# Second feed-forward: seven block products in place of eight in its second product

## The chip, the cores and the metric

One core of one Trainium2 chip runs the whole program in a single launch. The metric is the device time of that launch in microseconds (us): three runs of the kernel before took 784.38, 786.24 and 786.41 us, median 786.24.

## The reference

Three stages run one after the other on 2304 tokens (4 batches of 576) of width 512. The first is windowed and dilated attention, the second a feed-forward with a cosine. The third is the one that matters here:

```python
def _moe2_ref(x, w1, w2, w3, w_out):          # x 2304 x 512, w1..w3 512 x 768, w_out 768 x 512
    h = np.maximum(np.maximum(x @ w1, x @ w2), x @ w3)
    return (h @ w_out).astype(np.float32)
```

Below, "the second feed-forward" is this function, "its first product" is the three products with w1, w2 and w3, and "its second product" is `h @ w_out`.

## The kernel before, in words

Every float32 operand of a matmul is split into two rounded parts, hi and lo, and a product takes three passes: hi x hi, lo x hi, hi x lo (`PASSES`, L445). ScalarE makes hi by a cast (`CAST`), VectorE makes lo by a subtraction; the helper `split` (L636) issues both. Each VectorE, ScalarE and TensorE queue runs its instructions in the order that a scheduler gave them when the program was built, so an instruction that waits holds up all that stand behind it on its engine.

The second feed-forward (`ff2`, L893) works on three blocks `t` of 768 tokens, cut into two halves of 384 (`HALF`). The 768 hidden features are six chunks of 128, taken in pairs: `f` = 0, 1, 2 is a pair, `r` = 0, 1 a chunk of it. Per block there are nine steps `q`, three per pair (one for each of w1, w2, w3).

- First product (`product`, L775). Each step is a 2 x 2 block product (two chunks of features, two halves of tokens) and is already done by seven block products in place of eight: sums A11, S1 ... of weight blocks, sums B11, T1 ... of input blocks, results gathered in the PSUM banks X, V and Y (`SUMS`, L611). Each of the seven is 6 matmuls of 128x384. `post` and `put` take them out of PSUM: ScalarE copies `s` and `v`, VectorE adds and takes the maximum in `mx`. After the third weight of a pair, `put` splits the maximum into a tile `g`, one for each chunk and token half (L818).
- Second product (`acc2`, L840). Output features are four groups `dm` of 128. For each `dm`, each token half `n` and each pair `f`, six matmuls of 128x384 (two chunks, three passes) accumulate in one of the banks 94 to 97 of the built program. That is 24 steps of 6 matmuls per block: 4 x 2 x 3. After the last pair ScalarE copies the bank to `o` and a DMA writes it out (L854). The first three steps fill holes in the block's last step `q`; the other 21 stand alone. While they run, ScalarE and VectorE make the next block's B sums (`b_make`, tiles `bt` and `ring`).
- Weights of the second product. `o_weights` (L743) loads a raw pair of chunks (512 KB, tile `raw`) into free slots of the weight pool and splits each chunk into a tile `w`. The scheduler places these six splits in the last part of the first feed-forward.

The first feed-forward ends with `acc_chunk` (L547, matmuls at L551), which reads the tiles `gt`: ScalarE casts their hi (L214), VectorE subtracts their lo (L542). These tiles come from the pool `gp`, which has two buffers (tag `g`).

Of the kernel before, what the change touches and what calls it, by code (L numbers as in the profile page):

```python
# [8 lines left out]
F32 = mybir.dt.float32  # L9
F32R = mybir.dt.float32r  # L10
# [4 lines left out]
ALU = mybir.AluOpType  # L15
# [3 lines left out]
B, H, S, D = 4, 8, 576, 64  # L19
# [12 lines left out]
NF2 = FF2 // 128  # L32
# [7 lines left out]
HALF = 384  # L40
# [124 lines left out]
def body(  # L165
# [11 lines left out]
    nc = tc.nc  # L177
# [45 lines left out]
    acc = bank[:4]  # L223
# [220 lines left out]
    g = {}  # L444
    PASSES = ((0, 0), (1, 0), (0, 1))  # L445
# [225 lines left out]
    def a_part(q, n):  # L671
        if q >= NB2 * NQUAD:
            return
        cols = 256 * len(PARTS[n])
        made = q < NQUAD and q not in PRE
        dt = F32R if made else F32
        if n < 3:
            w = slot_tile(3 + n + q % 2 * 3, [128, 2, cols], dt, "wa")
        else:
            w = wx.tile([128, 2, cols], dt, tag="x", name="wa")  # L680
        if made:
            if n == 0:
                x = raws[q][:, 0]
            elif n == 3:
                x = raws.pop(q)[:, 1, 256:]
            else:
                x = sums[q].rearrange("p a n -> p (a n)")[:, 512 * n - 512 : 512 * n]
            split(w, x, nc.gpsimd)
            kept[q, n] = w.bitcast(F32)
        else:  # L690

            nc.sync.dma_start(out=w, in_=kept_at(q % NQUAD, n))
            w = w.bitcast(F32R)
        for k, name in enumerate(PARTS[n]):
            ops.setdefault(q, {})[name] = w[:, :, 256 * k : 256 * k + 256]
# [45 lines left out]
    wo = {}  # L741

    def o_weights(f):  # L743

        if f % 2 == 0:
# [43 lines left out]
    taken = {}  # L789
    mx = {}  # L790
    g2 = {}
# [7 lines left out]
    def put(q, r, n, name, to):  # L799

        f, j = QUADS[q % NQUAD]
        x = bank_of(q)[to][:, :HALF]
        if j == 0 and (f, r) not in mx:
            mx[f, r] = slot_tile(10 + f % 2 * 2 + r, [128, 2, HALF], F32, "mx")
        m = mx[f, r][:, n]
        if name is None:
            if j == 0:
                nc.scalar.copy(m, x)
            else:
                nc.vector.tensor_tensor(out=m, in0=x, in1=m, op=ALU.max)  # L810
        else:
            y = taken.pop((q, name))
            o = m if j == 0 else y
            nc.vector.tensor_tensor(out=o, in0=y, in1=x, op=ALU.add)  # L814
            if j:
                nc.vector.tensor_tensor(out=m, in0=m, in1=y, op=ALU.max)  # L816
        if j == 2:
            g = slot_tile(14 + f * 4 + r * 2 + n, [128, 2, HALF], F32R, "g2")  # L818
            split(g, m, nc.vector)
            g2[f, r, n] = g  # L820
            if (r, n) == (1, 0):
                del mx[f, 0], mx[f, 1]

    def post(q, p):
        if p == 1:
# [11 lines left out]
        if p == 4:  # L837
            put(q, 1, 0, None, "X")

    def acc2(t, dm, n, f):  # L840

        a = acc[(2 * dm + n) % 4][:, :HALF]
        for r in range(2):
            for k, (x, y) in enumerate(PASSES):
                nc.tensor.matmul(  # L845
                    a,
                    wo[2 * f + r][:, x, 128 * dm : 128 * dm + 128],
                    g2[f, r, n][:, y],
                    start=f == 0 and r == 0 and k == 0,
                    stop=f == NF2 // 2 - 1 and r == 1 and k == 2,  # L850
                )
        if f == NF2 // 2 - 1:
            o = ptp.tile([128, HALF], F32, tag="pt", name="o")
            nc.scalar.copy(o, a)  # L854
            t0 = (2 * t + n) * HALF
            nc.sync.dma_start(out=outT[dm, :, t0 : t0 + HALF], in_=o)
# [93 lines left out]
    at = [0, 0, 0, 0, 0]  # L950
# [61 lines left out]
    n = len(first)  # L1012
# [347 lines left out]
```

## Time and profile before

| what | value |
|---|---|
| median of three runs | 786.24 us (784.38 to 786.41) |
| the profiled execution, its own time | 783.48 us |
| its span, first to last instruction | 781.7 us |
| TensorE (PE) busy | 757.8 us (97%) |
| VectorE (DVE) busy | 537.7 us (69%) |
| ScalarE (ACT) busy | 429.1 us (55%) |
| mean granted TensorE clock | 0.998 |
| second product, matmuls (L845) | 432, busy 76.3 us |
| first product, matmuls (L780) | 1134, busy 198.7 us |

The profile is of one execution; all durations below come from it. Matmuls are pipelined, so the time of one is read from the step between neighbours and not from its own 334 ns. The second feed-forward runs from about 504 us to the end.

### The profile page before, as it was taken

What the parts mean: (1) busy time and instruction counts of PE and PEld (TensorE: products, weight loads), DVE (VectorE), ACT (ScalarE), POOL (GpSimd) and SP (SyncE); (2) the same over time, 40 slices, a digit from 0 to 9 for tenths busy, and PEclk for the clock granted to TensorE, in tenths of its full rate; (3) what the DMA queues carried; (4) which work ended last, traced back from release to release, by engine and by line L of the source; (5) the groups of instructions that cost most, each with busy time, mean ns of one, the idle gap of its engine ahead of it and who ended that gap; (6) DMA issues with size and microseconds to landing.
All of it is one profiled execution on the core that took longest, in us unless ns stands there. A gap on an engine that the chain in (4) does not pass through costs nothing.

```text
span 781.7 us, 13197 instructions
## 1 busy us (share of the span) xinstructions
PE 757.8 (97%) x4592; PEld 668.4 (86%) x4592; DVE 537.7 (69%) x1416; ACT 429.1 (55%) x1046; POOL 114.4 (15%) x114
## 2 busy tenths in 40 slices
PE   7788999999999999999999999999999999999997
PEld 6566878778878778877788889999999999999997
DVE  6999998876875787677877759955463555625540
ACT  7879999678763767664544535533343332433311
POOL 2334231411121101100112212000200000000000
PEclk9999999999999999999999999999999999999999
DMA  9983111342333543223646562487755878368702
GB/s 347 417 323 123 36 58 51 103 151 97 123 120 133 163 137 118 97 79 115 213 178 209 212 229 112 156 281 243 260 182 165 257 242 257 100 194 254 241 13 81
DMA packets 60402, 134.28 MB, mean 172 GB/s; under 512 B 6704, under 2 KB 21168, under 8 KB 60336
## 3 DMA queue, kind: packets, MB, share of 16 engines
q1 hardware_dynamic: 60336, 133.44, 51.0%
q8 instruction: 36, 0.59, 0.3%
q14 instruction: 30, 0.25, 0.1%
HBM read 101.17 MB, written 32.24 MB: 171 GB/s over the span
## 4 chain that ended last, share of the span: by engine, by line
PE 68%; DVE 14%; DMA 7%; ACT 5%; issue 2%; POOL 2%; SPq 1%; POOLq 0%; DVEq 0%; ACTq 0%
PE bank L780 25%; PE bank L452 15%; PE bank L551 14%; PE bank L845 9%; DMA rawp<-wd 2%; PE bank L341 2%; ACT e L291 2%; PE bank L410 2%; DVE wx L263 2%; DVE e L385 2%; PE bank L393 1%; POOL lo L735 1%; DMA raw<-wd 1%; DMA x1d<-o 1%; DMA opd<-hi 1%
## 5 line engine op out<-in xcount | busy, mean ns | idle before, releaser
L452 PE MATMUL bank<-ring,w 128*128 128x512 f32 (+1 forms) x960 | 218.6, 374 | 2.7 <-ACT ring L214 2.7
L551 PE MATMUL bank<-gt,w 128*128 128x512 f32 (+1 forms) x960 | 216.7, 372 | 3.5 <-DVE o L564 1.8
L780 PE MATMUL bank<-ring,wa 128*128 128x384 f32 x1134 | 198.7, 334 | 0.0
L551 PEld LDWEIGHTS bank<-gt,w 128*128 128x128 f32 x960 | 166.4, 189 | 35.7 <-DVE o L564 2.5
L780 PEld LDWEIGHTS bank<-ring,wa 128*128 128x128 f32 x1134 | 196.6, 188 | 0.4 <-ACT s L796 0.4
L452 PEld LDWEIGHTS bank<-ring,w 128*128 128x128 f32 x960 | 165.5, 189 | 35.6 <-ACT ring L214 3.5
L291 ACT ACTIVATE r<-r,hpi 128x512 f32<-128x512 f32 (+1 forms) x80 | 54.6, 683 | 54.6 <-DVE r L531 25.2
L291 ACT ACTIVATE e<-e,m 96x128 f32<-96x128 f32 x192 | 75.0, 393 | 4.4 <-DVE m L351 4.2
L845 PE MATMUL bank<-g,w 128*128 128x384 f32 x432 | 76.3, 334 | 0.0
L845 PEld LDWEIGHTS bank<-g,w 128*128 128x128 f32 x432 | 75.0, 188 | 0.0
L814 DVE TENSOR_TENSOR s<-s,bank 128x384 f32<-128x384 f32 x36 | 20.0, 554 | 49.0 <-PE bank L780 49.0
L796 ACT COPY s<-bank 128x384 f32<-128x384 f32 x54 | 25.9, 482 | 48.1 <-PE bank L780 47.9
L351 DVE CUSTOM_DVE_ANT_0 e<-bank,cs 96x128 f32<-96x128 f32 x192 | 42.7, 281 | 12.3 <-PE bank L341 12.2
L291 ACT ACT_TABLE_LOAD x38 | 48.8, 1283 | 1.4 <-PEq L1346 0.7
L507 POOL TENSOR_TENSOR gt<-r,gt 128x512 fp32r<-128x512 f32 x25 | 35.6, 1423 | 65.7 <-DVE gt L214 35.8
L210 POOL TENSOR_SCALAR gt<-r 128x512 fp32r<-128x512 f32 x25 | 16.4, 656 | 175.4 <-PE bank L551 117.1
L638 ACT CAST g<-mx 128x384 fp32r<-128x384 f32 x36 | 18.6, 516 | 41.6 <-DVE mx L816 26.8
L282 POOL TENSOR_TENSOR w<-wx,w 128x512 fp32r<-128x512 f32 x23 | 31.5, 1375 | 54.2 <-DVE w L214 45.2
L255 ACT ACTIVATE wh<-wh 128x256 f32<-128x256 f32 x48 | 20.7, 433 | 32.9 <-DMA wh<-in_w 20.5
L385 DVE TENSOR_TENSOR e<-e,z 96x512 f32<-96x512 f32 x48 | 36.8, 796 | 1.0
L291 ACT ACTIVATION_READ_ACCUMULATOR e<-e,m 96x1 f32 x192 | 36.4, 189 | 0.0
L496 DVE TENSOR_TENSOR r<-bank,r 128x512 f32<-128x512 f32 x47 | 32.2, 684 | 5.5 <-ACT r L291 5.3
(83 smaller groups left out, 856.6 us busy)
## 6 DMA issues: line engine op xcount, KB each, us to landing
wa<-opd SPq DMA_DIRECT2D x72, 512.0 KB, 4.5
qkv<-in_qkv SPq DMA_DIRECT2D x48, 336.0 KB, 4.2
wh<-in_w SPq DMA_DIRECT2D x36, 256.0 KB, 2.8
w<-in_w_in SPq DMA_DIRECT2D x16, 512.0 KB, 8.6
w<-in_w_out SPq DMA_DIRECT2D x16, 512.0 KB, 9.2
wa<-opd SPq DMA_DIRECT2D x24, 256.0 KB, 4.3
wd<-wh SPq DMA_DIRECT2D x36, 128.0 KB, 1.8
opd<-hi SPq DMA_DIRECT2D x18, 256.0 KB, 2.1
```

The costliest lines, as they stand in the source:

```text
L255: nc.scalar.activation(high, high, AF.Prelu, scale=2.0**-112, alpha=2.0**32)
L282: eng.tensor_tensor(out=w[:, 1, :], in0=words.pop(key), in1=w[:, 0, :].bitcast(F32), op=ALU.subtract)
L291: last_table.append(nc.scalar.activation(*args, **kw).ins)
L351: nc.vector.tensor_tensor_reduce(out=e[:, 2 * j + h, :], in0=places_of[j, h], in1=mask[:, kind, :], scale=-1.0 / math.sqrt(D), scalar=3e38 ...
L385: eng.tensor_tensor(out=e, in0=e, in1=z[:, n, :].unsqueeze(2).to_broadcast([QB, 4, KB]), op=ALU.mult)
L452: pe(nc.tensor.matmul(hv, w[:, a, 128 * c : 128 * c + 128], ring[c][:, x, c0 : c0 + n_tok], start=n == 0 and j == 0, stop=n == NC - 1 and ...
L496: nc.vector.tensor_tensor(out=r, in0=hv, in1=r, op=ALU.mult)
L507: eng.tensor_tensor(out=gt[:, 1, :], in0=r, in1=gt[:, 0, :].bitcast(F32), op=ALU.subtract)
L551: pe(nc.tensor.matmul(a_dm, w[:, a, 128 * dm : 128 * dm + 128], gt[:, x, :], start=first and n == 0, stop=last and n == 2,))
L780: nc.tensor.matmul(out, ops[q][a][:, x, 128 * c : 128 * c + 128], b_op(b, c)[:, y], start=first and c == 0 and n == 0, stop=c == 1 and n == 2,
L796: nc.scalar.copy(x, bank_of(q)[to][:, :HALF])
L845: nc.tensor.matmul(a, wo[2 * f + r][:, x, 128 * dm : 128 * dm + 128], g2[f, r, n][:, y], start=f == 0 and r == 0 and k == 0, stop=f == NF2 ...
```

## The change

For the pairs `f` = 0 and 1 the second product is also a 2 x 2 block product: two halves of the 512 output features by two token halves, over the two chunks. It now goes by seven block products, each for two groups `m` of 128 output columns. The third pair is done as before and is added in the same banks.

Three things come with it. Sums of the blocks of `w_out` (S1 to S4) are made on chip, once, in `o_weights`, from a raw tile that now sits in the pool `gp`. Sums T1 to T4 of the blocks of `h` are made in every block by `g_sum`, at the places of `G_AT`. And `acc2` now has steps of two kinds: `P1` to `P7` are the seven products, `Lin` is the third pair for output half `i` and token half `n`. After some steps a bank is taken out of PSUM while it is still in use: `P1`, `P5`, `P6` are copied to `taken` by ScalarE, `P7` is added to the copy of `P5` by VectorE, and `L00`, `L01`, `L11` add a `taken` tile to the bank on VectorE. `L10` is a ScalarE copy.

```diff
     def o_weights(f):
+        wo[f] = slot_tile(26 + f, [128, 2, 512], F32R, "w")
+        k, r = divmod(f, 2)
+        raw = raws["o"]
+        if k not in SEVEN:
+            split(wo[f], raw[:, r], nc.vector)
+            return
...
+            split2(of("A11"), a11)
+            s1 = sp.tile([128, 256], F32, tag="e", name="ws")
+            nc.vector.tensor_tensor(out=s1, in0=a21, in1=a22, op=ALU.add)
+            split2(of("S1"), s1)
+            nc.vector.tensor_tensor(out=a21, in0=a11, in1=a21, op=ALU.subtract)
+            split2(of("S3"), a21)
+            nc.vector.tensor_tensor(out=a11, in0=s1, in1=a11, op=ALU.subtract)
+        else:
+            split(wo[f], raw[:, 1], nc.vector)
...
+            split2(of("S2"), a11)
+            nc.vector.tensor_tensor(out=a12, in0=a12, in1=a11, op=ALU.subtract)
+            split2(of("S4"), a12)
+    def o_load(f):
         if f % 2 == 0:
-            raws["o"] = slot_tile(22 + f // 2, [128, 2, 512], F32, "raw")
+            raws["o"] = gp.tile([128, 2, 512], F32, tag="g", name="raw")
             nc.sync.dma_start(out=raws["o"], in_=wod[f // 2])
-        wo[f] = slot_tile(26 + f, [128, 2, 512], F32R, "w")
-        split(wo[f], raws["o"][:, f % 2], nc.vector)
...
+    def split2(hl, x):
+        nc.scalar.copy(hl[0], x)
+        nc.vector.tensor_tensor(out=hl[1], in0=x, in1=hl[0].bitcast(F32), op=ALU.subtract)
+    SEVEN = (0, 1)
...
         if j == 2:
-            g = slot_tile(14 + f * 4 + r * 2 + n, [128, 2, HALF], F32R, "g2")
-            split(g, m, nc.vector)
-            g2[f, r, n] = g
+            if f in SEVEN:
+                name = f"B{r + 1}{n + 1}"
+                g_raw[f, name] = m
+                if name != "B12":
+                    g_op[f, name] = g_tile(f, r * 2 + n)
+                    split2(g_op[f, name], m)
+            else:
+                g2[f, r, n] = g_tile(f, r * 2 + n)
+                split2(g2[f, r, n], m)
...
+    G_AT = ((3, -1), (3, -2), (4, -1), (4, -2), (6, -2), (7, 3), (7, 7), (8, 3))
...
+        nc.vector.tensor_tensor(out=out, in0=g_raw[f, x], in1=g_raw[f, y], op=ALU.subtract)
...
+        split2(g_op[f, name], out)
...
+    def acc2(t, m, kind):
+        a, b, c, d = (acc[x][:, :HALF] for x in range(4))
+        X, V, Y, Z = (a, b, c, c) if m == 0 else (d, b, a, c)
+        if kind[0] == "P":
+            to, w, x, first = SUMS[int(kind[1])]
+            to = {"X": X, "V": V, "Y": Y}[to]
+            steps = [(o_op[f, w], g_op[f, x], m) for f in SEVEN]
...
+        if kind in ("P1", "P5", "P6"):
+            x = tmp.tile([128, HALF], F32, tag="r", name="taken")
+            nc.scalar.copy(x, to)
+            taken[m, kind] = x
+        elif kind == "P7":
+            x = taken[m, "P5"]
+            nc.vector.tensor_tensor(out=x, in0=x, in1=to, op=ALU.add)
...
-    ACCS = [(dm, n, f) for d in (0, 2) for fs in ((0, 1), (2,)) for dm in (d, d + 1) for n in range(2) for f in fs]
+    ACCS = [(0, k) for k in ("P1", "P5", "P2", "P6", "P3")] + [(1, "P1")]
+    ACCS += [(0, k) for k in ("P7", "L01", "L00", "P4", "L10", "L11")]
+    ACCS += [(1, k) for k in ("P5", "P6", "P2", "P3", "P7", "L01", "L00", "P4", "L10", "L11")]
...
+                    if p == 3 and 0 < q <= NF2:
+                        o_load(q - 1)
                     if p == 7 and 0 < q <= NF2:
                         o_weights(q - 1)
+                    if (q - first, p) in G_AT:
+                        g_sum()
```

The scheduler's order moves at two places. The first is where the first feed-forward ends and the second begins. On TensorE it stood like this before (L551 is the first feed-forward's last work, L780 the first product of the second; banks 94 to 97 are its four accumulators):

```order
L551 MATMUL bank_97<-gt,w 128x256 x3
L780 MATMUL bank_98<-ring_149,wa 128x384 x3
L780 MATMUL bank_98<-ring_150,wa 128x384 x3
L780 MATMUL bank_100<-ring_149,wa 128x384 x3
L780 MATMUL bank_100<-ring_150,wa 128x384 x3
L551 MATMUL bank_94<-gt,w 128x256 x2
L780 MATMUL bank_101<-ring_151,wa 128x384 x2
L551 MATMUL bank_94<-gt,w 128x256
L551 MATMUL bank_95<-gt,w 128x256 x3
L551 MATMUL bank_96<-gt,w 128x256 x3
L551 MATMUL bank_97<-gt,w 128x256 x3
```

Now the same work stands so (L825 is what was L780):

```order
L551 MATMUL bank_94<-gt,w 128x256 x3
L551 MATMUL bank_95<-gt,w 128x256 x3
L551 MATMUL bank_96<-gt,w 128x256 x3
L551 MATMUL bank_97<-gt,w 128x256 x3
L825 MATMUL bank_98<-ring_149,wa 128x384 x3
L825 MATMUL bank_98<-ring_150,wa 128x384 x3
L825 MATMUL bank_100<-ring_149,wa 128x384 x3
L825 MATMUL bank_100<-ring_150,wa 128x384 x3
L825 MATMUL bank_101<-ring_151,wa 128x384 x3
L825 MATMUL bank_101<-ring_152,wa 128x384 x3
L825 MATMUL bank_98<-ring_149,wa 128x384 x3
L825 MATMUL bank_98<-ring_150,wa 128x384 x3
```

Fourteen matmuls of the first product that stood between and inside the last two groups of L551 now stand behind them.

At the same place ScalarE's queue held only copies out of PSUM before (`s` and `v`, which the next products on the same bank wait for); the splits `w<-raw` stood further ahead, among the last `gt` casts:

```order
L638 CAST ring_150<-bt_5437 128x384
L796 COPY s_5477<-bank_98 128x384
L796 COPY v_5485<-bank_100 128x384
L796 COPY s_5501<-bank_98 128x384
L796 COPY s_5518<-bank_99 128x384
L796 COPY v_5536<-bank_100 128x384
L808 COPY mx<-bank_98 128x384
L796 COPY s_5561<-bank_99 128x384
L796 COPY s_5581<-bank_98 128x384
L796 COPY v_5604<-bank_100 128x384
```

Now the splits of the `w_out` blocks stand among these copies. `w<-raw` and `whole` are casts of raw blocks and of their sums; the first `w<-raw` waits for the first raw pair, the third (128x256) for the second pair:

```order
L841 COPY s_5477<-bank_98 128x384
L789 CAST w<-raw 128x256
L638 CAST w<-raw 128x512
L841 COPY v_5485<-bank_100 128x384
L789 CAST whole<-ws 128x256
L789 CAST whole<-raw 128x256
L789 CAST w<-raw 128x256
L841 COPY s_5501<-bank_98 128x384
L638 CAST w<-raw 128x512
L789 CAST whole<-raw 128x256
L841 COPY s_5518<-bank_99 128x384
```

and some steps later, where `w<-raw` x2 waits for the third raw pair:

```order
L789 CAST whole<-raw 128x256 x2
L853 COPY mx<-bank_98 128x384
L841 COPY s_5561<-bank_99 128x384
L789 CAST w<-raw 128x256
L638 CAST w<-raw 128x512 x2
L841 COPY s_5583<-bank_98 128x384
L841 COPY v_5618<-bank_100 128x384
L841 COPY s_5645<-bank_98 128x384
```

Copies `s` and `v` now stand behind casts that wait for a transfer. On VectorE the matching subtractions stand among the adds that empty the same banks.

The second place is the stretch with second-product steps only. Before, on ScalarE (`g` are the third pair's tiles, `ring` the next block's B sums, `o` the outputs):

```order
L638 CAST g_6088<-mx 128x384
L638 CAST g_6107<-mx 128x384
L638 CAST g_6131<-mx 128x384
L638 CAST ring_149<-x1raw 128x384
L638 CAST ring_149<-bt 128x384
L638 CAST ring_151<-x1raw 128x384
L638 CAST ring_149<-bt 128x384
L854 COPY o<-bank_94 128x384
L638 CAST ring_151<-x1raw 128x384
L854 COPY o<-bank_95 128x384
```

Now (`whole` is what `g` was, `taken` are the copies out of banks still in use):

```order
L789 CAST whole<-mx 128x384 x2
L953 COPY taken<-bank_94 128x384
L638 CAST ring_149<-x1raw 128x384
L638 CAST ring_149<-bt 128x384
L953 COPY taken<-bank_97 128x384
L638 CAST ring_151<-x1raw 128x384
L638 CAST ring_149<-bt 128x384
L638 CAST ring_151<-x1raw 128x384
L638 CAST ring_149<-bt 128x384
L961 COPY o<-bank_94 128x384
```

The `taken` copies stand between the casts `ring` of the next block's sums; the steps that go on in the same bank depend on them.

## Rows read from the trace of the kernel before

**Rows 1.** The page, parts 1 and 2: busy time and the granted TensorE clock.
```profile
PE 757.8 (97%) x4592; PEld 668.4 (86%) x4592; DVE 537.7 (69%) x1416; ACT 429.1 (55%) x1046; POOL 114.4 (15%) x114
...
PEclk9999999999999999999999999999999999999999
```

**Rows 2.** Chain of waits by time, 520 us to the end: start, us, what.
```profile
596.61 63.44 PE bank L780 x366
...
755.73 19.77 PE bank L845 x114
...
775.57 0.49 ACT o L854
...
776.08 1.86 DMA outT<-o
...
778.04 0.48 ACT o L854
```

**Rows 3.** The page, part 5: the second feed-forward's second product.
```profile
L845 PE MATMUL bank<-g,w 128*128 128x384 f32 x432 | 76.3, 334 | 0.0
```

**Rows 4.** Waits of PE from 500 us on: total, times, longest.
```profile
PE bank L551 <- DVE gt L542: 0.6, 1, 0.6
```

**Rows 5.** Timeline of PE where the stages meet: start, us, what, idle before.
```profile
498.48 3.45 PE L551 MATMUL bank<-gt,w 128*128 128x256 f32 x26
502.53 1.46 PE L551 MATMUL bank<-gt,w 128*128 128x256 f32 x10 [0.60 <-DVE gt L542]
503.83 2.25 PE L780 MATMUL bank<-ring,wa 128*128 128x384 f32 x12
506.17 0.50 PE L551 MATMUL bank<-gt,w 128*128 128x256 f32 x2
...
508.04 4.14 PE L780 MATMUL bank<-ring,wa 128*128 128x384 f32 x21
```

**Rows 6.** Timeline of VectorE and ScalarE, same stretch.
```profile
499.86 0.69 DVE L639 TENSOR_TENSOR w<-raw,w 128x512 fp32r<-128x512 f32 x1
...
503.53 1.29 DVE L639 TENSOR_TENSOR w<-raw,w 128x512 fp32r<-128x512 f32 x2
503.65 0.51 ACT L291 ACTIVATE r<-r,hpi 128x256 f32<-128x256 f32 x1 [1.24 <-DVE r L531]
...
505.20 0.43 DVE L540 TENSOR_TENSOR r<-bank,r 128x256 f32<-128x256 f32 x1
...
505.71 0.41 ACT L214 CAST gt<-r 128x256 fp32r<-128x256 f32 x1 [0.61 <-DVE r L540]
...
506.15 0.42 DVE L542 TENSOR_TENSOR gt<-r,gt 128x256 fp32r<-128x256 f32 x1
```

**Rows 7.** Transfers: KB each, median us; then min, median, max for wa, 512 to 522 us.
```profile
wa<-opd SPq DMA_DIRECT2D x72, 512.0 KB, 4.5
...
raw<-wod SPq DMA_DIRECT2D x3, 512.0 KB, 6.0
...
DMA to landing us min/median/max: 4.0/4.3/4.7
```

**Rows 8.** Groups by shape, 510 to 660 us: busy, mean ns, idle before.
```profile
L796 ACT COPY s<-bank 128x384 f32<-128x384 f32 x35 | 16.8, 482 | 31.0 <-PE bank L780 30.9
L814 DVE TENSOR_TENSOR s<-s,bank 128x384 f32<-128x384 f32 x23 | 12.8, 554 | 31.6 <-PE bank L780 31.6
L639 DVE TENSOR_TENSOR g<-mx,g 128x384 fp32r<-128x384 f32 x21 | 11.7, 558 | 10.1 <-ACT g L638 9.4
L638 ACT CAST g<-mx 128x384 fp32r<-128x384 f32 x21 | 10.8, 516 | 22.2 <-DVE mx L816 14.3 <-DVE mx L810 7.8
...
L638 ACT CAST wa<-raw 128x256 fp32r<-128x256 f32 x1 | 0.4, 411 | 0.0
```

**Rows 9.** Timeline of ScalarE in the first product-free stretch.
```profile
577.48 0.52 ACT L638 CAST ring<-bt 128x384 fp32r<-128x384 f32 x1 [1.15 <-DVE bt L768]
...
596.05 0.48 ACT L854 COPY o<-bank 128x384 f32<-128x384 f32 x1 [0.95 <-DMA outT<-o]
```

More of the change, by code (lines that the diff above doesn't have):

```diff
@@ L743, in o_weights, with whole @@
     def o_weights(f):
+        wo[f] = slot_tile(26 + f, [128, 2, 512], F32R, "w")
[4 more added lines that the diff above has]
+            return
+        a11, a21, a12, a22 = (raw[:, i, 256 * n : 256 * n + 256] for i in range(2) for n in range(2))
+        of = lambda name: o_op[k, name]
+        if r == 0:
+            o_op[k, "A11"] = [wo[f][:, x, :256] for x in range(2)]
+            o_op[k, "S4"] = [wo[f][:, x, 256:] for x in range(2)]
+            for n, name in enumerate(("S1", "S2", "S3")):
+                o_op[k, name] = [
+                    whole(14 + 6 * k + 2 * n + x)[:, 768:] for x in range(2)
+                ]
+            split2(of("A11"), a11)
[7 more added lines that the diff above has]
+            split(wo[f], raw[:, 1], nc.vector)
+            o_op[k, "A12"] = [wo[f][:, x, :256] for x in range(2)]
+            o_op[k, "A22"] = [wo[f][:, x, 256:] for x in range(2)]
+            split2(of("S2"), a11)
+            nc.vector.tensor_tensor(out=a12, in0=a12, in1=a11, op=ALU.subtract)
+            split2(of("S4"), a12)
+    def o_load(f):
         if f % 2 == 0:
-            raws["o"] = slot_tile(22 + f // 2, [128, 2, 512], F32, "raw")
+            raws["o"] = gp.tile([128, 2, 512], F32, tag="g", name="raw")
             nc.sync.dma_start(out=raws["o"], in_=wod[f // 2])
-        wo[f] = slot_tile(26 + f, [128, 2, 512], F32R, "w")
-        split(wo[f], raws["o"][:, f % 2], nc.vector)
+    wholes = {}
+    def whole(n):
+        if n not in wholes:
+            wholes[n] = slot_tile(n, [128, 1024], F32R, "whole")
+        return wholes[n]
+    def split2(hl, x):
+        nc.scalar.copy(hl[0], x)
+        nc.vector.tensor_tensor(out=hl[1], in0=x, in1=hl[0].bitcast(F32), op=ALU.subtract)
+    SEVEN = (0, 1)
+    o_op = {}
+    g_op = {}
     braw = {}
@@ L817, in put, with g_tile, g_sum @@
         if j == 2:
-            g = slot_tile(14 + f * 4 + r * 2 + n, [128, 2, HALF], F32R, "g2")
-            split(g, m, nc.vector)
-            g2[f, r, n] = g
+            if f in SEVEN:
[7 more added lines that the diff above has]
+                split2(g2[f, r, n], m)
             if (r, n) == (1, 0):
                 del mx[f, 0], mx[f, 1]
+                if f in SEVEN:
+                    g_todo.extend((f, name) for name in ("T1", "T2", "T3", "T4"))
+    G_AT = ((3, -1), (3, -2), (4, -1), (4, -2), (6, -2), (7, 3), (7, 7), (8, 3))
+    g_raw = {}
+    g_todo = []
+    T_AT = {(0, "T1"): 15, (0, "T2"): 0, (0, "T3"): 1, (0, "T4"): 9, (1, "T1"): 19, (1, "T2"): 2}
+    def g_tile(f, n):
+        t = whole(14 + 4 * f + n)
+        return [t[:, :HALF], t[:, HALF : 2 * HALF]]
+    def g_sum():
+        if not g_todo:
+            return
+        f, name = g_todo.pop(0)
+        x, y, to = {
+            "T1": ("B12", "B11", "B11"),
+            "T2": ("B22", "T1", "T1"),
+            "T3": ("B22", "B12", "B12"),
+            "T4": ("B21", "T2", "B21"),
+        }[name]
+        out = g_raw[f, to]
+        nc.vector.tensor_tensor(out=out, in0=g_raw[f, x], in1=g_raw[f, y], op=ALU.subtract)
+        g_raw[f, name] = out
+        at = T_AT.get((f, name))
+        if at in (15, 19):
+            g_op[f, name] = g_tile(f, 1)
+        else:
+            t = slot_tile(at, [128, 2, HALF], F32R, "gs") if at is not None else gp.tile([128, 2, HALF], F32R, tag="g", name="gs")
+            g_op[f, name] = [t[:, 0], t[:, 1]]
+        split2(g_op[f, name], out)
     def post(q, p):
@@ L838, in post @@
             put(q, 1, 0, None, "X")
[L840 to L844, printed above, removed]
-                nc.tensor.matmul(
[L846 to L850, printed above, removed]
-                )
-        if f == NF2 // 2 - 1:
-            o = ptp.tile([128, HALF], F32, tag="pt", name="o")
-            nc.scalar.copy(o, a)
+    def acc2(t, m, kind):
[5 more added lines that the diff above has]
+            steps = [(o_op[f, w], g_op[f, x], m) for f in SEVEN]
+        else:
+            i, n = int(kind[1]), int(kind[2])
+            to, first = {"00": (Y, False), "01": (V, False), "10": (X, False), "11": (Z, True)}[kind[1:]]
+            steps = [
+                ([wo[2 * f + r][:, x] for x in range(2)], g2[f, r, n], 2 * i + m)
+                for f in range(NF2 // 2)
+                if f not in SEVEN
+                for r in range(2)
+            ]
+        for k, (w, x, at) in enumerate(steps):
+            for j, (p, y) in enumerate(PASSES):
+                nc.tensor.matmul(
+                    to,
+                    w[p][:, 128 * at : 128 * at + 128],
+                    x[y],
+                    start=first and k == 0 and j == 0,
+                    stop=k == len(steps) - 1 and j == 2,
+                    skip_group_check=not first,
+                )
+        if kind in ("P1", "P5", "P6"):
[5 more added lines that the diff above has]
+            nc.vector.tensor_tensor(out=x, in0=x, in1=to, op=ALU.add)
+        elif kind[0] == "L":
+            o = ptp.tile([128, HALF], F32, tag="pt", name="o")
+            if kind == "L10":
+                nc.scalar.copy(o, to)
+            else:
+                x = taken.pop((m, {"L00": "P1", "L01": "P6", "L11": "P5"}[kind]))
+                nc.vector.tensor_tensor(out=o, in0=x, in1=to, op=ALU.add)
```

2 lines of the change are left out of this document (1 added, 1 removed).

## Prediction

> **What bounds the kernel now.** I read the busy shares first. TensorE is busy 97% of the span, VectorE 69%, ScalarE 55%, and the granted clock is full in every slice [rows 1]. Because a busy TensorE is not a TensorE at its peak, I then followed the chain of waits in order of time. From 520 us to the end it lies on TensorE without a break, product after product, and leaves it only for the last outputs [rows 2]. TensorE's own list of waits says the same: from 500 us on it has one entry, 0.6 us, where the stages meet [rows 4]. So the second feed-forward is as long as its matmuls. One 128x384 matmul of the second product takes 19.77 / 114 = 0.173 us, of the first product 63.44 / 366 = 0.173 us [rows 2], so a step of six is 1.04 us. A matmul less is worth 0.173 us, as long as nothing new makes TensorE wait.
>
> **What goes.** Per block the second product had 24 steps; now it has 14 (seven products, two column groups) and 8 for the third pair, 22 in all. Two steps of six matmuls in three blocks are 36 of the 432 matmuls [rows 3], and 36 x 0.1733 = 6.24 us, all on the path.
>
> **The end.** The last output's copy starts at 778.04, because it needs a buffer that a transfer of 1.86 us from 776.08 still holds; that transfer follows the copy at 775.57 [rows 2]. That copy came 0.07 after its step, which ended at 755.73 + 19.77 = 775.50; two steps later, at 777.58, TensorE was done, so the last copy is 0.39 late. In the new order the last two outputs use buffers filled two and three steps before, and the wait goes; the last output is a VectorE add (0.55) in place of a ScalarE copy (0.48) [rows 8]. Together -0.32 us, between -0.39 and +0.07.
>
> **Where the stages meet.** Before, fourteen matmuls of the first product filled TensorE while it waited for the last `gt` tiles, and at 508.04 all of L551 and these fourteen were done [rows 5]. Now L551 comes first and has no filler. But five subtractions for `w`, 0.60 us apart (two take 1.29, one 0.69), stood ahead of the last `gt` subtraction at 506.15 [rows 6], and they leave too. I moved the rows up one by one: the last sine starts at 502.5 in place of 503.65, the product after it at 503.1 (505.20), the hi cast at 503.5 (505.71), the last lo is done at 504.4 (506.57). TensorE then ends L551 at 505.67; fourteen matmuls, 2.43 us, make 508.10. That is +0.06 us. If the casts left behind held VectorE fully it would be 506.57 + 1.20 + 2.43 = 510.2, +2.2 us; if TensorE never waited, 503.83 + 1.44 + 2.43 = 507.7, -0.3. I take +0.06, since VectorE's rows there stand end to end.
>
> **The raw blocks of w_out.** This is the new wait. The three loads went into free slots and had nothing to wait for. Now they use the two buffers of the `gt` tiles: the first can start when the second-to-last group of L551 is through, about 503.6 (503.83 before [rows 5], less a wait that shrinks by some 0.25), the second after the last group, 505.75, the third when the first raw pair has been used up. ScalarE's copies `s` and `v` stand behind the casts that wait for them, and an engine's queue does not pass a waiting instruction: ScalarE idled 0.95 us before an output's copy, for a transfer [rows 9]. The Trainium skill says this as a rule (PSUM — Partial Sum Buffer, Engine vs sequencer instructions): the queues of ScalarE, VectorE and GpSimd are strictly first in, first out; the trace agrees.
>
> With L for the time from issue to landing, the first pair is there at 503.6 + L. Two casts and the copy `v` (0.48) end 1.5 us later; the casts are 0.41 for 256 columns and, with 0.52 for 384, 0.62 for 512 [rows 8]; TensorE wants that bank for its fifth product, at 505.67 + 4 x 1.04 = 509.83. So this costs nothing up to L = 4.7. The second pair, at 505.75 + L, holds the copy of the fourth product, due two steps later: free up to L = 5.2. The third pair is the tightest. By the order of the queues the first pair is used up at 514.6 (L = 4.3), so the third lands at 518.9; the cast, its subtraction, a maximum, two sums and the add that frees the bank end 2.9 us later, 521.8, and TensorE wants it at 522.3. An L longer by 1 us moves this by 2, as the third load starts later too: free up to L = 4.5.
>
> What is L? Loads of the same size took 4.0 to 4.7 us in this stretch, median 4.3, and 4.5 over the kernel; the raw loads took 6.0, but three were issued within 2 us of each other [rows 7]. At 4.3 the stalls are nothing, at 4.7 about 0.5, at 5.0 about 1.2, at 6.0 about 3.2 us. I take 4.7, the upper end of the stretch itself: +0.5 us, bounds 0 and 3.3.
>
> The Trainium skill (DMA: Bandwidth & Descriptors, Anatomy of one DMA) fits the time of one transfer from GpSimd as 2.0 us plus its bytes at 436 GB/s, an estimate of 3.2 us for 512 KB. The rows show 4.0 at the least, so the trace does not bear it out for these loads; by the page the stall would be nothing and the sum 0.5 us better.
>
> **The new work on VectorE and ScalarE.** Per block VectorE gets eight sums T, six more lo subtractions and eight adds out of banks, 22 x 0.555 = 12.2 us, and ScalarE six more casts (0.52) and as many copies as before [rows 8]. In the steps with the first product the copies and adds that TensorE needs have two steps, 2.08 us, and take 0.48 or 0.55; I went through the order at the densest place (four casts for T2, T3, B22 and B21 in a row): the copy behind them ends 1.1 us before it is due. In the stretch with second-product steps alone, the new waits have the same two steps: `P6`'s copy before `P7`, `P7`'s add before `P4`, `L00`'s add before `L11`, and in the second half `P5`'s copy before `P3`. That is seven a block, 21 in all. Their queue neighbours are the `ring` casts, which wait 1.15 us each for VectorE [rows 9]; in the order as it stands a `taken` copy has at most one such link in front that is not done by then. I put them at nothing. If the cover is gone, a wait with one such link (1.15 + 0.52) ahead costs 0.07 + 1.67 + 0.55 - 2.08 = 0.21 us, with two 1.88 us (0.07 is the gap from a step's end to its copy, as at the end). No gain can come from this part. The weight sums, once, lie in the same queues as the raw loads and are in the times above.
>
> **The sum.** -6.24 - 0.32 + 0.06 + 0.5 = -6.0 us. Against the profiled execution's 783.48 that is 777.5 us. The median of the runs, 786.24, is 2.8 us above it, and the forecast is for the median: 786.24 - 6.0 = 780.2 us. With every term at its better bound it is -6.24 - 0.39 - 0.3 = -6.9, with every one at its worse -6.24 + 0.07 + 2.2 + 3.3 = -0.7 us.
>
> **Rivals.**
> - Late raw blocks. The loads land after 5.5 to 6 us, as raw loads did [rows 7], since other 512 KB loads run beside the third; the stalls are 2.4 to 3.3 us and the time 782.1 to 783.2. For it: the `raw` row. Against it: they are now issued one by one, 2 us and 9 us apart. Chance 0.18.
> - The bare handover. VectorE does not use the time that the `w` subtractions leave, TensorE idles for the last `gt` tile, and the gain shrinks by 2.2 to 782.4. Against it: those rows stand end to end before that tile. Chance 0.05.
> - The bank waits replace the matmuls saved. The 21 waits of the lone steps become the bound: `taken` copies and adds behind the `ring` chain. With one link ahead of each, 21 x 0.21 = 4.4 us, leaving 784.6, no change (chance 0.08). With two links ahead of a third of them, 7 x 1.88 = 13.2 us: 793.4, slower (chance 0.04). It costs the whole gain from 6.0 / 21 = 0.29 us a wait, and shows as slower from (6.0 + 2.4) / 21 = 0.40. For it: ScalarE and VectorE wait for each other there link by link [rows 9]. Against it: TensorE waited for neither in the kernel before [rows 4], and in the built order no more than one link stands ahead.
> - That the change does not do what it says could only mean that matmuls are not saved; the built program has 396 in place of 432, so I leave this out.
>
> **Numbers.** My forecast has 0.65, late blocks 0.18, the bare handover 0.05, the bank waits 0.12. What a measurement of this kernel can tell from no change is about 0.3%, 2.4 us, so faster means below 783.9. The forecast and the handover count as faster, late blocks for 0.14 of their 0.18, the rest as the same: faster 0.84, same 0.12, slower 0.04. The range goes from 777.9 (the lowest run, 784.38, less 6.5) to 784.2 (late blocks and 1 us of the runs' own spread); outside are the bank waits and little else.
>
> **What would show it.** Right: 396 matmuls on the second product's line, 0.173 us each; each block two steps, 2.08 us, shorter; TensorE waiting in the first 20 us of the second feed-forward alone, for ScalarE's `v` copy or VectorE's add, under 1 us together; the last output's copy with no wait for a transfer. Wrong: waits of TensorE for `taken` or `o` in each of the three lone stretches, waits over 2 us behind `w<-raw`, or a granted clock below full after such a gap.

## The result

The changed kernel takes 780.65 us, median of 14 runs (776.5 to 784.27), the kernel before in the same comparison 786.25 us (784.38 to 791.55, 14 runs). The ratio is 0.9912, 95% interval 0.9895 to 0.993: 6.9 us less, between 5.5 and 8.3. The forecast was 780.2 us, 6.0 us less than before.

Its profiled execution took 781.46 us, with a span of 779.7 us. First the page: busy time of the engines, and the granted clock in 40 slices.

```profile
PE 755.8 (97%) x4556; PEld 665.0 (85%) x4556; DVE 570.0 (73%) x1498; ACT 438.5 (56%) x1072; POOL 115.0 (15%) x114
...
PEclk9799999999999999999999999999999999999999
```

Against [rows 1] VectorE has gained 32 us of busy time, and TensorE has lost 2 only. The clock row has a dip in its second slice that [rows 1] has not. It lies in code that the change does not touch. TensorE is busy for longer there, and late: the same group of twelve L452 matmuls starts at 49.85 us before and at 52.77 us now. A further 1.9 us are lost between 424 and 440 us, where the same instructions stand in the same order; TensorE waits there for VectorE, 0.81 us at the longest, and no run here tells why (over the other profiled kernels this stretch is 0.05 to 2.0 us longer than before). So I compare a stretch that begins behind both and whose start is the same instruction in every kernel: from the last L452 group of the first feed-forward to the end of the span. It starts at 501.81 us here and at 497.04 us in the kernel before, in both two rows ahead of the last L551 group but one (x10). TensorE's timeline of the kernel before, ahead of [rows 5], and then that of the changed kernel where the stages meet (start, us, what, idle before):

```profile
497.04 1.60 PE L452 MATMUL bank<-ring,w 128*128 128x256 f32 x12
```

```profile
501.81 1.60 PE L452 MATMUL bank<-ring,w 128*128 128x256 f32 x12
...
507.04 1.45 PE L551 MATMUL bank<-gt,w 128*128 128x256 f32 x10 [0.51 <-DVE gt L542]
508.74 1.92 PE L551 MATMUL bank<-gt,w 128*128 128x256 f32 x12 [0.25 <-ACT gt L214]
510.50 63.61 PE L825 MATMUL bank<-ring,wa 128*128 128x384 f32 x366
```

That is 781.7 - 497.04 = 284.66 us before and 779.7 - 501.81 = 277.89 us now, 6.77 us less. Whether a part of the 1.9 us belongs to the change is not shown; the ratio, which covers the whole launch, leaves at most 6.8 - 5.5 = 1.3 us for it. From 510.50 on TensorE has no gap: 366 matmuls of the first product in one row, and no later row of its timeline has a wait. Its list of waits (total, times, longest) ends where the second feed-forward starts:

```profile
PE bank L551 <- DVE gt L542: 0.5, 1, 0.5
PE bank L551 <- ACT gt L214: 0.2, 1, 0.2
```

The chain of waits, by time, is then TensorE's alone up to the last output:

```profile
599.06 63.44 PE bank L825 x366
...
756.10 19.78 PE bank L943 x114
...
775.90 0.55 DVE o L964
```

From the second block's long row of the first product to the third block's lone stretch it is 756.10 - 599.06 = 157.04 us; before it was 755.73 - 596.61 = 159.12 [rows 2]. One block's second product lies between, and the difference, 2.08 us, is two steps of six.

Where the 6.77 us are from:

| term | forecast | measured | read from |
|---|---|---|---|
| matmuls, 3 x 2.08 | -6.24 | -6.24 | 157.04 against 159.12 us |
| where the stages meet | +0.06 | +0.12 | 510.50 + 2.43 - 501.81 = 11.12, before 508.04 - 497.04 = 11.00 |
| raw loads of w_out | +0.5 | 0 | no wait behind them |
| new VectorE and ScalarE work | 0 | 0 | no wait behind it |
| the end | -0.32 | -0.30 | 779.7 - 775.88 = 3.82, before 781.7 - 777.58 = 4.12 |
| a stall of the kernel before that I had missed | none | -0.36 | below |

The missed stall: in the kernel before, the 352 matmuls from 508.04 took 61.53 us to the end of the row. In the changed kernel 366 take 63.61, which is 366 x 0.1733 + 0.16; 352 would be 61.17. The rest, 0.36, hides inside a row: TensorE's matmuls show no wait there, but its weight loads (PEld) do.

```profile
PEld bank L780 <- ACT s L796: 0.4, 1, 0.4
```

Now the transfers, as in [rows 7], for the raw blocks (microseconds from issue to landing), and then ScalarE's and VectorE's timelines at the tightest place, where the third load is waited for:

```profile
DMA to landing us min/median/max: 3.1/4.3/4.5
```

```profile
522.14 0.48 ACT L841 COPY s<-bank 128x384 f32<-128x384 f32 x1 [0.56 <-PE bank L825]
...
523.87 1.14 ACT L638 CAST w<-raw 128x512 fp32r<-128x512 f32 x2 [0.95 <-DMA raw<-wod]
...
526.27 0.55 DVE L859 TENSOR_TENSOR v<-v,bank 128x384 f32<-128x384 f32 x1
```

The loads took 3.1, 4.3 and 4.5 us, within the cover of 4.7, 5.2 and 4.5 us that the prediction had worked out. The add at 526.27 frees the bank at 526.82; TensorE wants it 96 matmuls after 510.50, at 527.14. So 0.32 us were left at the tightest place: hidden, but only just. The estimate of 3.2 us from the Trainium skill (DMA: Bandwidth & Descriptors, Anatomy of one DMA) fits the first load; the other two took a third and two fifths longer.

### The profile page after: what moved, and what is told of

The parts are those of the page before. It is cut to its first block, busy times and chain, and to the rows that moved or that the text cites. A ratio compares the mean times of both kernels' runs of the same rounds, so it can differ in the third digit from the quotient of the medians.

```text
span 779.7 us, 13244 instructions
## 1 busy us (share of the span) xinstructions
PE 755.8 (97%) x4556; PEld 665.0 (85%) x4556; DVE 570.0 (73%) x1498; ACT 438.5 (56%) x1072; POOL 115.0 (15%) x114
## 4 chain that ended last, share of the span: by engine, by line
PE 68%; DVE 13%; ACT 8%; DMA 7%; issue 2%; SPq 1%; POOL 1%; POOLq 0%; DVEq 0%; ACTq 0%
PE bank L825 25%; PE bank L452 15%; PE bank L551 14%; PE bank L943 9%; ACT e L291 3%; PE bank L341 2%; DMA rawp<-wd 2%; PE bank L410 2%; PE bank L393 2%; DVE e L385 1%; ACT r L291 1%; DMA x1d<-o 1%; DVE wx L263 1%; ACT L291 1%; DMA opd<-hi 1%
## 5 line engine op out<-in xcount | busy, mean ns | idle before, releaser
L452 PE MATMUL bank<-ring,w 128*128 128x512 f32 (+1 forms) x960 | 220.2, 376 | 3.2 <-ACT ring L214 2.1
L551 PE MATMUL bank<-gt,w 128*128 128x512 f32 (+1 forms) x960 | 216.6, 372 | 3.9 <-DVE o L564 1.9
L825 PE MATMUL bank<-ring,wa 128*128 128x384 f32 x1134 | 198.0, 334 | 0.0
L452 PEld LDWEIGHTS bank<-ring,w 128*128 128x128 f32 x960 | 166.4, 190 | 36.9 <-ACT ring L214 2.4
L551 PEld LDWEIGHTS bank<-gt,w 128*128 128x128 f32 x960 | 166.3, 189 | 36.0 <-DVE o L564 2.5
L825 PEld LDWEIGHTS bank<-ring,wa 128*128 128x128 f32 x1134 | 196.6, 188 | 0.0
L943 PE MATMUL bank<-whole,w 128*128 128x384 f32 x252 | 47.5, 334 | 0.0
L943 PEld LDWEIGHTS bank<-whole,w 128*128 128x128 f32 x252 | 44.0, 188 | 0.0
L789 ACT CAST whole<-mx 128x384 fp32r<-128x384 f32 x36 | 18.5, 514 | 27.6 <-DVE mx L861 14.8
```

The costliest lines, as they stand in the source:

```text
L452: pe(nc.tensor.matmul(hv, w[:, a, 128 * c : 128 * c + 128], ring[c][:, x, c0 : c0 + n_tok], start=n == 0 and j == 0, stop=n == NC - 1 and ...
L551: pe(nc.tensor.matmul(a_dm, w[:, a, 128 * dm : 128 * dm + 128], gt[:, x, :], start=first and n == 0, stop=last and n == 2,))
L825: nc.tensor.matmul(out, ops[q][a][:, x, 128 * c : 128 * c + 128], b_op(b, c)[:, y], start=first and c == 0 and n == 0, stop=c == 1 and n == 2,
L943: nc.tensor.matmul(to, w[p][:, 128 * at : 128 * at + 128], x[y], start=first and k == 0 and j == 0, stop=k == len(steps) - 1 and j == 2, s ...
```

## The experiments

All are read on the same stretch, from the last L452 group to the end of the span (277.89 us in the changed kernel), since the start of the program moves total times by more than most of these differences. Line numbers of the kernels differ by one to seven.

**One pair instead of two.** `SEVEN = (0,)` in place of `SEVEN = (0, 1)`.

> The changed kernel with one pair of chunks by seven products in place of two (pair 0; pairs 1 and 2 go as the third pair did): 414 matmuls of the second product, between 432 and 396. Read on the stretch from the start of the first feed-forward's last L452 group to the end of the span: 284.66 us in the kernel before, 277.89 in the changed one. Theory (only the number of matmuls counts): 18 matmuls x 0.1733 = 3.12 us more than the changed kernel, 281.0 us, no wait of TensorE that was not there, and a time about 3.1 us above the changed kernel's. Rival (the gain came from the new order, the moved loads and the adds at the end, not from matmuls): 277.9 us again. Rival (the new work has a price hidden by other things, which falls with half of it gone): under 280.5 us.

Measured: 781.1 - 500.18 = 280.92 us, 3.03 more than the changed kernel. Median 782.92 us (10 runs), ratio to the kernel before 0.9946, interval 0.9924 to 0.9968: between the two kernels. The chain lies on TensorE as before, with a longer lone stretch:

```profile
576.09 22.36 PE bank L943 x129
```

129 matmuls in 22.36 us are 0.1733 each. The number of matmuls decides; both rivals fall.

**The moved loads alone.** The kernel before, with only this:

```diff
-            raws["o"] = slot_tile(22 + f // 2, [128, 2, 512], F32, "raw")
+            raws["o"] = gp.tile([128, 2, 512], F32, tag="g", name="raw")   # now in o_load
...
+                    if p == 3 and 0 < q <= NF2:
+                        o_load(q - 1)
```

> The kernel before with one thing of the change alone: the raw blocks of w_out are loaded into the pool gp, later, and split at the start of the second feed-forward; the second product keeps its 432 matmuls. Theory (the moved loads cost TensorE nothing, the place where the stages meet +0.1, and a stall of 0.36 us that the kernel before had at its first product goes): 284.66 + 0.12 - 0.36 = 284.4 us for the stretch, no wait behind the raw loads. Rival of the prediction (late raw blocks): +2.4 us, 287. Rival (a part of the gain came from the moved loads): 283.5 or less.

Measured: 786.1 - 501.90 = 284.20 us, 0.46 less than before, expected 0.24 less. TensorE's timeline:

```profile
501.90 1.60 PE L452 MATMUL bank<-ring,w 128*128 128x256 f32 x12
...
510.58 63.61 PE L782 MATMUL bank<-ring,wa 128*128 128x384 f32 x366
```

The handover is 510.58 + 2.43 - 501.90 = 11.11 us (+0.11), the 366 matmuls take 63.61 again, so the stall of 0.36 is gone, and the remaining 0.2 lies behind the last output. The moved loads cost nothing by themselves. With them the scheduler leaves out the filler here too, as in the changed kernel, so the stall goes with that order and not with the seven products. ScalarE's timeline of the kernel before shows where it came from:

```profile
508.24 0.63 ACT L638 CAST w<-raw 128x512 fp32r<-128x512 f32 x1 [0.37 <-PE bank L551]
...
509.45 0.48 ACT L796 COPY s<-bank 128x384 f32<-128x384 f32 x1
```

P1, one of the fillers, was through at 503.83 + 1.04 = 504.87, but its copy `s` began 4.6 us later, behind a cast that had waited for L551. The filler had its price: TensorE needed that bank before ScalarE's queue had come to the copy.

**The bank waits without cover.** P7 directly behind P6:

```diff
-    ACCS = [(0, k) for k in ("P1", "P5", "P2", "P6", "P3")] + [(1, "P1")]
+    ACCS = [(0, k) for k in ("P1", "P5", "P2", "P6", "P7", "P3")] + [(1, "P1")]
```

and the same for group m = 1; TensorE's matmuls of the second product are kept in this order. In the changed kernel two steps lie between P6 and P7 (of the text below, the first sentence says one and the theory two). Its timeline shows them: P6 ends where this row starts, and P7 starts at 582.26.

```profile
580.18 2.24 PE L943 MATMUL bank<-whole,w 128*128 128x384 f32 x12
```

> The changed kernel with P7 directly behind P6 (the two use the same bank, and ScalarE must have copied P6's result before P7 may write); in the changed kernel a step of six lies between them. Group m = 0 has no matmul left between the two in any block, group m = 1 has four of the first product in blocks 0 and 1 and none in block 2. Theory (these waits cost nothing because two steps, 2.08 us, cover a copy that starts 0.07 after its step): without cover a wait of 0.6 to 0.8 us (0.07 + 0.48 + the restart) at four places and 0 to 0.2 at two, in all 2.4 to 3.6 us on the stretch of 277.89 us: 280.3 to 281.5. Rival (the copies come late, one or two casts that wait 1.15 us stand in front): 1.7 us or more at each place, 8 us or more in all. Rival (the cover is irrelevant): 277.9.

Measured: 782.0 - 500.32 = 281.68 us, 3.79 more, just above the upper end. TensorE's waits (total, times, longest) and its timeline at the first of the four places, then ScalarE's there:

```profile
PE bank L943 <- ACT taken L953: 2.3, 4, 0.6
```

```profile
577.66 1.21 PE L943 MATMUL bank<-gs,whole 128*128 128x384 f32 x6
579.43 1.31 PE L943 MATMUL bank<-gs,whole 128*128 128x384 f32 x6 [0.57 <-ACT taken L953]
580.59 4.32 PE L943 MATMUL bank<-whole,w 128*128 128x384 f32 x24
...
589.95 0.86 PE L825 MATMUL bank<-ring,wa 128*128 128x384 f32 x4
590.73 1.31 PE L943 MATMUL bank<-gs,whole 128*128 128x384 f32 x6
```

```profile
578.45 0.51 ACT L789 CAST whole<-mx 128x384 fp32r<-128x384 f32 x1 [1.67 <-DVE mx L855]
578.90 0.48 ACT L953 COPY taken<-bank 128x384 f32<-128x384 f32 x1
```

P6's six matmuls are through at 577.66 + 1.04 = 578.70, P7 starts at 579.43, 0.73 later. (I count from starts and 0.1733 a matmul, here and below; the idle time in a row is shorter, since the length of a row holds the tail of its last matmul.) The copy began 0.20 after P6, where the prediction had 0.07, because one cast stood in front; and P7 itself then took 1.16 in place of 1.04. That makes 0.85 a place, 3.4 for four; the two places with four fillers lose 0.2 each. So this wait is real, and the two steps of six between P6 and P7 hide all of it; the other waits of the lone stretches were not bared. One link stood in front of the copy, as the prediction had it, and was nearly done.

**VectorE loaded further.** `split2` of the blocks of h and of their sums does its subtraction twice.

> The changed kernel with every lo subtraction of the blocks of h and of their sums done twice, so 18 more VectorE instructions of 0.56 us a block, some 10 us a block, 30 us in all, most of it in the steps of the first product. Theory (the new work on VectorE lies beside TensorE, with 1.1 us to spare at the densest place): TensorE waits for under 1 us a block, the stretch of 277.89 us becomes 277.9 to 280.9. Rival (VectorE is as good as full there, and the changed kernel stands at the edge): most of the 30 us comes through, 295 us or more.

Measured: 778.6 - 499.26 = 279.34 us, 1.45 more for 30 us of work. There is one wait, in block 0, where the weights are still being prepared:

```profile
507.95 53.40 PE L826 MATMUL bank<-ring,wa 128*128 128x384 f32 x306
562.37 10.70 PE L826 MATMUL bank<-ring,wa 128*128 128x384 f32 x60 [1.01 <-DVE mx L860]
```

306 matmuls from 507.95 end at 560.98, and TensorE goes on at 562.37, 1.39 later, more than the 1 us a block that was expected. In blocks 1 and 2 another 10 us of VectorE work each cost nothing. So VectorE is not the bound there.

**Longer landing of the raw loads.** `nc.gpsimd.dma_start` in place of `nc.sync.dma_start` for the raw blocks.

> The changed kernel with the three raw loads of w_out issued by GpSimd in place of SyncE, to change L, the time from issue to landing (3.1, 4.3 and 4.5 us in the changed kernel, without a wait of TensorE). TensorE's order is the same; some casts and subtractions of the weight sums move by a place or two. Theory (TensorE waits only for loads that take longer than 4.7, 5.2 and 4.5 us; beyond that the third pair costs two us for each us): with L up to 4.5 no wait and 277.9 us for the stretch from the start of the last L452 group; at 5.0 about 1.2 us, at 6.0 about 3.2 us more, all of it in the first 20 us of the second feed-forward. Rival (the loads have far more cover than the prediction gave them): no wait at 6 us either. Rival (the queue of the issuing engine decides, not L): waits with L under 4.5.

Measured: 785.6 - 501.00 = 284.60 us, 6.71 more: the whole gain is gone. TensorE's timeline, the two ScalarE copies that it waited for, and the landing times:

```profile
509.68 4.33 PE L825 MATMUL bank<-ring,wa 128*128 128x384 f32 x24
516.39 9.65 PE L825 MATMUL bank<-ring,wa 128*128 128x384 f32 x54 [2.38 <-ACT v L841]
528.69 51.74 PE L825 MATMUL bank<-ring,wa 128*128 128x384 f32 x288 [2.66 <-ACT s L841]
580.28 1.20 PE L943 MATMUL bank<-whole,w 128*128 128x384 f32 x6
```

```profile
515.86 0.48 ACT L841 COPY v<-bank 128x384 f32<-128x384 f32 x1 [2.88 <-DMA x1d<-o]
...
527.64 0.62 ACT L638 CAST w<-raw 128x512 fp32r<-128x512 f32 x1 [3.33 <-DMA raw<-wod]
528.17 0.47 ACT L841 COPY s<-bank 128x384 f32<-128x384 f32 x1
```

```profile
DMA to landing us min/median/max: 4.3/6.3/6.9
```

The second wait is of the kind that the prediction described: the third load, issued at 521.30, is used at 527.64, 6.3 us later; a cast waits for it with the s copy behind it, and TensorE stands from 525.75 (516.39 + 54 x 0.1733) to 528.69, 2.94 us. But it is not at the prediction's place. In the changed kernel this s copy (522.14, in the result above) stands ahead of the third pair's casts (523.87); here one of them has moved ahead of it. In the changed kernel's order a landing at 527.64 would have cost some 1.7 us, an estimate: the add that frees the bank ended 2.95 after the cast there, which makes 530.59, and TensorE would want the bank at 509.68 + 96 x 0.1733 + 2.55 = 528.87. The prediction had 3.2 for 6.0 us. The first wait, 2.55 us, I had not expected: the v copy waited for a buffer that a store of the first feed-forward's output still held (SyncE's four stores took 6.1 to 6.7 us to land here, 1.8 to 3.9 in the changed kernel). The third part is the clock. TensorE's busy time and clock by stretch, columns us, busy time and count of PE, PEld, DVE, ACT and POOL, granted clock, DMA share, GB/s:

```profile
516.00:526.00 10.00, 9.61 (x54) 9.32 (x54) 7.94 (x20) 5.85 (x15) 0.53 (x1) 1.00 0.83 287
...
530.00:532.00 2.00, 2.00 (x8) 2.00 (x7) 2.00 (x6) 0.00 (x0) 0.00 (x0) 0.50 0.11 12
532.00:534.00 2.00, 2.00 (x13) 2.00 (x13) 1.58 (x4) 0.48 (x1) 0.00 (x0) 0.97 0.81 252
```

After the stand of 2.94 us the granted clock was 0.50 between 530 and 532 us, the lower of the two levels, and 0.97 again from 532. The 288 matmuls from 528.69 took 51.59 us where 49.91 are due: 1.68 us. After the first stand, 2.55 us, it stayed at 1.00. In sum 2.55 + 2.94 + 1.68 = 7.17, and 0.44 less behind the last output. So late raw blocks, the prediction's likeliest rival, do stop TensorE, here for 2.94 us with 1.68 us of low clock behind it; that they would have cost what it said in the changed kernel's own order is not shown. TensorE waited nowhere for the first load, of 4.3 us, so nothing speaks for the rival that the issuing queue decides. And a late load alone does not decide either: in the two kernels with fillers below, the third load was used 5.7 us (521.27 to 527.00) and 6.4 us (518.78 to 525.17) after its issue, and TensorE did not wait for it; its casts stand two copies later there than in the changed kernel.

**Filling the idle time where the stages meet.** P1 and P5 of step 0 ahead of the last L551 group; then P1 ahead of the second-to-last and P5 ahead of the last:

```diff
+        if s == NS + LAG - 1:
+            for p in (1, 5):
+                product(0, p, True)
```

> The changed kernel with the first two products (P1 and P5 of step 0, 2.08 us) set ahead of the last L551 group on TensorE. In the changed kernel TensorE stands idle there for 0.67 us before the second-to-last group can go on and for 0.50 us before the last. Theory of the handover (idle for the last gt tile is filled by work that is ready): 0.50 us shorter, 277.4 us. Theory of the raw loads' cover (from the prediction: the second load starts when the last group is through, now 1.58 us later, and the copies behind its casts are due 0.50 us earlier, against a cover of 0.9 us at L = 4.3): a wait of about 1 us for an s or v copy or an add behind w<-raw, and 278 to 279 us, no gain. If the first holds without a wait, the cover was larger than the prediction had it.

> The changed kernel with P1 of step 0 set ahead of the second-to-last L551 group and P5 ahead of the last, so that both idle times (0.67 and 0.50 us) are filled. Theory of the handover: 1.17 us shorter, 276.7 us for the stretch, the shortest of all kernels. Theory of the raw loads' cover: the first load starts 0.37 us later and its copy v is due 1.17 us earlier, with 1.15 us to spare in the changed kernel, so TensorE waits some 0.4 us; the second starts 0.9 us later, its copies are due 1.17 us earlier with 0.9 us to spare, some 1.2 us: 277 to 278.5 us, less than half of the gain or none. In time neither is more than 0.2% from the changed kernel, so the profile decides: ratio to the kernel before 0.989 to 0.993.

Measured: 778.6 - 500.51 = 278.09 us and 776.1 - 498.24 = 277.86 us, no gain in either. The second one's median is 779.05 us (6 runs), ratio to the kernel before 0.9907, interval 0.9875 to 0.9939, not to be told from the changed kernel's. Its timelines of TensorE and ScalarE:

```profile
498.24 1.60 PE L452 MATMUL bank<-ring,w 128*128 128x256 f32 x12
...
507.50 1.21 PE L825 MATMUL bank<-ring,wa 128*128 128x384 f32 x6
509.18 2.01 PE L825 MATMUL bank<-ring,wa 128*128 128x384 f32 x10 [0.46 <-ACT s L843]
511.45 58.88 PE L825 MATMUL bank<-ring,wa 128*128 128x384 f32 x338 [0.27 <-ACT v L843]
```

```profile
507.69 0.51 ACT L638 CAST ring<-bt 128x384 fp32r<-128x384 f32 x1 [1.09 <-DVE bt L813]
508.10 0.64 ACT L564 COPY o<-bank 128x256 f32<-128x256 f32 x2
508.63 0.49 ACT L843 COPY s<-bank 128x384 f32<-128x384 f32 x1
509.79 0.41 ACT L789 CAST w<-raw 128x256 fp32r<-128x256 f32 x1 [0.67 <-DMA raw<-wod]
...
510.93 0.47 ACT L843 COPY v<-bank 128x384 f32<-128x384 f32 x1
```

The idle time at the L551 groups is gone: 507.50 - 498.24 less 2.08 us of filler is 7.18, where the changed kernel needs 510.50 - 501.81 = 8.69. The 1.5 us came back: 0.64 before 509.18 and 0.54 before 511.45, both within the next four products, 0.14 inside the last row, and 0.16 behind the last output. The theory of the raw loads holds for the second wait only: the v copy stands behind casts, the first of which waited 0.67 us for a transfer. The s copy has no cast of a raw block ahead of it. P1 was through at 503.60, but its copy stands behind a cast that waited for VectorE and behind ScalarE's two output copies of the first feed-forward, which need the last L551 group. The Trainium skill's rule of queues that go first in, first out (PSUM — Partial Sum Buffer, Engine vs sequencer instructions) is what the rows show here: the copies start one behind the other.

**The same with the raw blocks out of the way.** One step later, and their casts pinned on ScalarE behind the copies:

```diff
-                    if p == 3 and 0 < q <= NF2:
-                        o_load(q - 1)
+                    if p == 3 and 1 < q <= NF2 + 1:
+                        o_load(q - 2)
...
-            split2(of("S1"), s1)
+            pin(split2(of("S1"), s1))
```

> The kernel with P1 and P5 of step 0 set ahead of the last two L551 groups (as in the one before, where the idle time went but casts of the raw blocks of w_out held ScalarE's s and v copies up for 1.3 us), with the loads and the splitting of w_out one step q later, and the casts of the raw blocks pinned on ScalarE behind the s and v copies that stand before them in the program. Theory (at this place TensorE waits only for copies that stand behind casts of raw blocks): neither the handover's 1.17 us nor a wait for s or v, 276.7 us for the stretch from the start of the last L452 group, against 277.9 for the changed kernel. Rival (the next thing is late at once: VectorE's sums of raw blocks, which are not pinned, or the casts for T2 to T4 behind the weight sums): a wait of 0.5 us or more for DVE mx, ACT s or ACT gs, 277.2 us or more. In time the first would be 0.15% better than the changed kernel, a ratio to the kernel before of about 0.990.

Measured: 781.4 - 501.69 = 279.71 us, 1.8 more than the changed kernel; median 781.95 us (12 runs), ratio 0.9927, interval 0.9904 to 0.9949. TensorE's waits:

```profile
PE bank L828 <- DVE mx L866: 0.9, 1, 0.9
PE bank L828 <- ACT v L846: 0.6, 1, 0.6
PE bank L828 <- ACT s L846: 0.5, 1, 0.5
```

The theory falls. The s copy is as late as before, without a raw block near it. The v copy now waits for VectorE, whose sum of raw blocks, not pinned, waited 0.71 us for its transfer; and the weight sums, moved later, meet those of the blocks of h at 559 us. No version that I tried is faster than the changed kernel by more than the measurement can tell.

## Why the prediction was right

- What bounds the kernel: TensorE's chain, so a matmul less is 0.173 us. Right, to the hundredth in the changed kernel; with one pair alone the stretch was 3.03 us longer, where 3.12 were expected.
- Where the stages meet: +0.06 forecast, +0.12 measured. The subtractions that left did make room: the place costs as much as before, without its filler.
- The raw blocks: the mechanism is right, the size is off. I took L = 4.7 us, and it was 3.1, 4.3 and 4.5, so the term of +0.5 was 0. That 1 us more of L moves the third pair by 2 is not borne out: the first load landed 1.2 us sooner than the 4.3 that I had reckoned with, and the third was still issued where I had it (519.33 less the 4.77 us by which this execution is late is 514.56; forecast 514.6). With 6.3 us, in another order, the wait came, 2.94 us; the prediction named a low clock after such a gap as a sign, but gave it no price. And the upper end of this rival, 783.2, is a slip: 3.3 in place of 0.5 makes 783.0.
- The new work on VectorE and ScalarE: nothing, as forecast. Without the two steps between P6 and P7 it is 0.85 us a place; in the order as it stands, nothing at all 21 places. This was the rival that could have eaten the gain.
- The end: -0.30 measured, -0.32 forecast, and only partly shown. The last copy, an add now, starts 0.02 us after TensorE in place of 0.46, and its wait for a transfer is gone, as forecast. But from that copy to the end it is 3.80 us now and was 3.66, and over all kernels here between 3.3 and 4.0, so the sum of this term has an uncertainty as large as itself.
- Missed: the stall of 0.36 us inside a row of the kernel before. I had read waits of matmuls only, not those of weight loads, so the price of the filler did not show.

The two misses, -0.5 and -0.36, have the same sign: the stretch gained 6.77 us, not 6.0. The medians differ by 5.6, and both figures lie in the interval of the ratio, so the runs' times cannot tell the two misses from none; the profile can. That the median, 780.65, lies within 0.5 us of the forecast is in part luck: on the stretch the forecast was 0.8 us off.

## What to carry to other kernels

Where one engine's chain is unbroken and one of its instructions has a known step, a change in their number could be priced to a few hundredths here; the risk lies in new waits, and each is decided by what stands in front of it in its engine's queue and by how many steps cover it. Idle time of the bounding engine is not free to be filled: look first at what is due next, since here 1.2 of 1.5 us of filled idle time came back within four products, from copies that stood behind the same work. And read the waits of weight loads beside those of matmuls: the stall of 0.36 us inside a long row showed there alone.

## What the runs showed of the hardware

The same program's runs differ by 1%, and the mean granted clock with them: the changed kernel's 14 runs go from 776.5 us at 0.998 to 784.27 us at 0.984. In the two profiled executions the clocks differ in the first 40 us, where both have the same code: from 20 to 40 us (columns as above) the clock was 0.97 before and 0.74 in the changed kernel.

```profile
0.00:20.00 20.00, 15.04 (x170) 12.29 (x170) 13.46 (x71) 14.94 (x60) 4.52 (x12) 0.94 0.92 349
20.00:40.00 20.00, 15.96 (x163) 11.53 (x160) 18.47 (x79) 16.98 (x71) 7.36 (x10) 0.97 1.03 417
```

```profile
0.00:20.00 20.00, 15.67 (x172) 12.48 (x174) 13.12 (x71) 14.83 (x60) 4.54 (x12) 0.91 0.92 346
20.00:40.00 20.00, 17.65 (x150) 13.27 (x151) 16.18 (x67) 14.60 (x61) 6.00 (x9) 0.74 1.03 417
```

In the 20 us ahead of that TensorE had been busy for 15.0 and 15.7 us. What decides whether the clock falls there, no run here tells. For the reader it means that two profiled executions are compared from a common instruction on, and not by their spans. And transfers of one size are not of one length: 512 KB from SyncE landed after 3.1 us and, in the same tile, after 6.4 us in the kernel with two fillers; which of the three loads was the slowest differed between the kernels.
